# Attention plus MLP block on one core: a tenth of the exps on VectorE, one GELU per chunk, Q projections moved, denser fillers

## The chip, the cores and the metric

The kernel runs on 1 core of a Trainium2 chip. The time is device microseconds of that core. Executions of the kernel before span 0.4% in the main comparison (1060.83 to 1064.96 us) and 1.1% in the widest batch (1062.11 to 1073.93 us). The profiler names the engines PE (TensorE), DVE (VectorE), ACT (ScalarE), POOL (GpSimd) and SP (SyncE); PEld is TensorE's weight load.

## The reference

One transformer block on 2048 tokens of width 640, with modulation rows computed from a vector `c`. In what follows, a score product is a part of q k^T, an exp is the exponential of the softmax on such scores, and P.V is the product of the exps with v.

```python
qkv = (x @ wqkv).reshape(B, S, 3, H, Dh)          # H = 32 heads, Dh = 20
scores = einsum('bhqd,bhkd->bhqk', q, k) * Dh ** -0.5
o = einsum('bhqk,bhkd->bhqd', softmax(scores), v); attn = o.reshape(B, S, D) @ wo
...
x = x + ga * attn(layernorm(x) * (1 + ca) + sa)
h = gelu(y @ w1 + b1)                              # tanh form, F = 1536; y = layernorm(...)
x = x + gb * (h @ w2 + b2)
```

## The kernel before

The kernel builds a list of operations with their dependences. A list scheduler at build time puts them into a fixed order for each engine, and the order is then emitted with semaphores. Queries go in four chunks of 512. A chunk has 8 groups of 4 heads and 16 key tiles, which makes 2048 score tiles of 128x512 in all. While chunk i is in attention, TensorE also does projections (chunk 0) or the output product and the MLP of chunk i-1.

Score products of three tiles fill three PSUM banks (0 to 2, then 3 to 5), and one exp of 1536 columns empties them into a ring in SBUF (slots that are used again once P.V has read them). P.V accumulates in bank 6. Every other product ("auxiliary") goes through bank 7.

```python
def score_unit(ts, b0, prio=1):
    ...                                            # K = 32 products, one per tile, into banks b0..b0+2
    acts.append(P.op("act", lambda e: e.activation(dst, src, ACTF.Exp, scale=SCALE),
                     R=[pb], W=[dst], dur=d, lat=d + 0.24, prio=4, name="exp"))
```

A filler is a product with zero weights that adds nothing. It is there to keep TensorE's clock up, and the scheduler puts one in when TensorE would wait and too few columns were streamed lately:

```python
if be == "pe" and self.filler is not None and gate and bt > free["pe"] + 0.06:
    ...
    if sum(x[1] for x in fl) < self.fill_min:      # 3500 columns in the last 3.413 us
        o = self.op("pe", self.filler[0], ...)     # 512 columns into bank 6
```

`gate` is true only between the first and the last P.V row of a group. GELU is done piecewise: VectorE forms the argument for 1024 columns, ScalarE does a Tanh, VectorE the product; six times in each of chunks 0 to 2. All Q projections are done in chunk 0:

```python
late = [J_proj(g, 0, t) for t in (1, 2, 3) for g in range(NG)]   # 24 jobs of 5 products
```

The softmax here doesn't subtract the row's maximum and nothing guards it: scores larger than these inputs give would overflow.

Of the kernel before, what the change touches and what calls it, by code (L numbers as in the profile page):

```python
# [10 lines left out]
ESZ = {BF16: 2, F32: 4}  # L11


class Op:
    __slots__ = ("eng", "emit", "strong", "weak", "dur", "lat", "prio", "rel", "idx",
                 "users", "dma", "nbytes", "name", "npred", "ready", "t0", "t1",
                 "inc", "cnt", "sem", "startusers", "mode", "order", "wc", "gate")


class Sched:  # L20
# [10 lines left out]
    def __init__(self, nc, es):  # L31
        self.nc = nc
        self.ops = []
        self.marks = []
        self.filler = None
        self.fill_min = 3500
        self.lw = {}
        self.rd = {}
        self.fp = {}
        self.sem = {e: es.enter_context(nc.semaphore("s_" + e))  # L40
                    for e in ("pe", "act", "dve", "pool")}
        self.dsem = [es.enter_context(nc.semaphore(f"dm{i}")) for i in range(self.NDSEM)]
        self.ndma = 0
        self.dlast = [None] * self.NDSEM
# [35 lines left out]
    def op(self, eng, emit, R=(), W=(), dur=0.1, lat=None, prio=5, rel=None, name="",  # L80
           dma=False, nbytes=0, mode=0, after=(), wc=0.0, gate=None):
# [4 lines left out]
        o.wc, o.gate = wc, gate  # L86
# [33 lines left out]
        o.strong, o.weak = strong, weak - strong  # L120
        self.ops.append(o)
# [3 lines left out]
    def schedule(self):  # L125
# [17 lines left out]
        lastmode = {e: None for e in engs}  # L143
        bw = 0.0
        ham = {}
        fl = []
        gate = False
# [6 lines left out]
        while left:  # L154
# [7 lines left out]
            if be == "pe" and self.filler is not None and gate and bt > free["pe"] + 0.06:  # L162

                f0 = free["pe"]
                while fl and fl[0][0] < f0 - self.TICK:
                    fl.pop(0)
                if sum(x[1] for x in fl) < self.fill_min:
                    o = self.op("pe", self.filler[0], dur=self.filler[1] / 2400.0, mode="f", name="fill",
                                wc=float(self.filler[1]))
                    o.npred = 0  # L170
                    o.ready = 0.0
                    left += 1
                    avail["pe"].append(o)
                    bt = f0
# [5 lines left out]
            if be == "pe":  # L180
# [5 lines left out]
                if o.gate is not None:  # L186
                    gate = o.gate
                d *= slow
                if lastmode[be] != o.mode:
# [108 lines left out]
def bass_adaLN_cond__mha_block__mixer_channel_mlp__prompt_kernel(  # L298
# [8 lines left out]
    GELU_C = math.sqrt(2.0 / math.pi)  # L307
    X2, OUT2 = A_x[0], out[0]
    VW, RING = 24, 15
    QS = [(0, 512), (512, 512), (1024, 512), (1536, 512)]  # L310
    FILL = 760

    es = ExitStack()
    with es:
        P = Sched(nc, es)
        arena = es.enter_context(nc.sbuf_tensor("arena", [128, 98304], BF16))
# [3 lines left out]
        def V(off, shape, dtype=BF16):  # L320
# [4 lines left out]
            assert off % 64 == 0 and off + nb <= 196608, (off, nb)  # L325
# [9 lines left out]
        def alloc(nbytes):  # L335
            o = top[0]
            top[0] += (nbytes + 63) // 64 * 64
            assert top[0] <= 196608, top[0]
# [9 lines left out]
        o_ring = alloc(RING * 512 * 2)  # L348
        o_ot = alloc(2 * NG * 512 * 2)
        o_wo = alloc(NG * D * 2)  # L350
        o_mlp = alloc(8192)
# [7 lines left out]
        ring = V(o_ring, [RING * 512])  # L359
# [7 lines left out]
        x1b = V(o_mlp, [2, 1024])  # L367
        gsq = V(o_mlp + 4096, [1024])
        gth = V(o_mlp + 6144, [1024])
# [7 lines left out]
        b2b = V(o_ot + 13312, [D])  # L377
# [3 lines left out]
        gbh = V(o_mlp + 5120, [D])  # L381
        gab = V(o_mlp + 6400, [D])
# [4 lines left out]
        arena_t_f32 = rinv.tensor  # L387
        sumt = V(alloc(64), [16])
        rsm = V(alloc(64), [16], F32)
        zero = V(alloc(256), [128])  # L390
        gbb2 = V(alloc(1280), [D])
        sbr = V(alloc(1280), [D])
# [10 lines left out]
        b1col = V(alloc(64), [KF], F32)  # L403

# [23 lines left out]
        def mm(outp, lhsT, rhs, start, stop, prio, n, rel=None, name="", cyc=None):  # L428
# [3 lines left out]
                        name=name, wc=n)  # L432
# [29 lines left out]
        def mmjob(outp, pairs, n, prio, pace, name):  # L462
            rels = pace.rels(len(pairs))
            for i, (l, r) in enumerate(pairs):
                mm(outp, l, r, i == 0, i == len(pairs) - 1, prio, n, rel=rels[i], name=name)
# [11 lines left out]
        for w in (1, 0):  # L477
# [28 lines left out]
             dur=0.22, lat=0.4, prio=0, mode="f", name="warm", wc=512, gate=True)  # L506
        P.filler = (lambda e: e.matmul(bank(6), zero, idr, start=False, stop=False, skip_group_check=True), 512)  # L507
# [85 lines left out]

        def proj_job(g, which, tc, prio, pace=NOPACE, eng="dve"):
            bb = bank(aux_bank())
            mmjob(bb, [(wqk[:, kt, which, g * 128:(g + 1) * 128], hT[:, kt, tc * 512:(tc + 1) * 512])
                       for kt in range(KD)], 512, prio, pace, "proj")
            d = kT[:, g, tc * 512:(tc + 1) * 512] if which == 1 else qT[:, tc, g, :]
            if eng == "act":
                act(d, bb, ACTF.Copy, prio=1)  # L600
            else:
                dve(lambda e: e.tensor_copy(d, bb), [bb], [d], 512, prio=2)  # L602
# [18 lines left out]
        acts = P.marks  # L621
# [8 lines left out]
        def score_unit(ts, b0, prio=1):  # L630
# [19 lines left out]
            def em(e):  # L650
                r = None
                for (o_, lh, rh, hl) in lst:
# [6 lines left out]
                 wc=0.25 * n * len(ts))  # L659
# [3 lines left out]
            acts.append(P.op("act", lambda e: e.activation(dst, src, ACTF.Exp, scale=SCALE),  # L663
                             R=[pb], W=[dst], dur=d, lat=d + 0.24, prio=4, name="exp"))

        def pv_row(ci, g, kt, split=False):
# [10 lines left out]
            def em(e):  # L677
                r = None
                for (o_, lh, rh, hl) in lst:
# [5 lines left out]
                 gate=True if kt == 0 else False if kt == TT - 1 else None)  # L685
# [22 lines left out]
        def sum_job(ci, g):  # L708
# [15 lines left out]
            dve(lambda e: e.tensor_tensor(d, d, rb, op=ALU.mult), [d, rb], [d], n, prio=3, name="div")  # L724

        def attention(ci, g, kts, pend, two=False):
            n = QS[ci][1]
            for kt in kts:
                for hl in range(4):
                    if pend and pend[0][0] != ci and QS[pend[0][0]][1] != n:  # L730
                        score_unit(list(pend), 3 * (flat[0] % 2))
                        flat[0] += 1
                        pend.clear()
                    pend.append((ci, g, kt, hl))
                    k = 2 if two else 3 * (512 // n)
                    if len(pend) == k:
                        score_unit(list(pend), (2 if two else 3) * (flat[0] % 2))
                        flat[0] += 1
                        pend.clear()
# [29 lines left out]
        def run_chunk(ci, groups, aux):  # L769
# [3 lines left out]
            u0 = len(acts)  # L773
# [7 lines left out]
            for g in groups:  # L781
                for kt in range(TT):
                    attention(ci, g, [kt], pend)
                    todo.append((ci, g, kt))
                    while todo and (todo[0] + (3,)) in slot_of:
                        pv_row(*todo.pop(0))
                    flush(len(acts) - u0 - 1)
# [3 lines left out]
        aux = []  # L791

# [3 lines left out]
        def row_mod(dst, wm, c0, pace, scale=1.0, plus=0.0):  # L796

            for (n0, nw) in ((0, 512), (512, 128)):
# [6 lines left out]

        pool(lambda e: e.memset(selz, 0.0), [selz], prio=7)
        sz = selz.rearrange("p (a b) -> p a b", b=32)
        pool(lambda e: e.affine_select(out=sz, in_=sz, compare_op=ALU.not_equal, fill=1.0, base=-DH,
                                       pattern=[[-32, 4], [0, 32]], channel_multiplier=1),
             [selz], [selz], dur=0.3, prio=7)  # L810
# [6 lines left out]
        flat[0] = 0  # L817
        UG = 64 / 3.0
# [34 lines left out]
        def J_group(g):  # L853
            return [J_proj(g, 1, 0), J_proj(g, 0, 0), J_proj(g, 1, 1), J_proj(g, 1, 2), J_proj(g, 1, 3)]

        late = [J_proj(g, 0, t) for t in (1, 2, 3) for g in range(NG)]
        spread(0.5, UG - 1, mix(J_group(2), J_v(160) + [J_row(gab, wm1, 0)]))
        spread(UG, 2 * UG - 1, mix(J_group(3), J_v(320) + [
            J_row(sbr, wm1, D), J_row(cb1, wm2, 0, plus=1.0), J_row(gbh, wm2, D, scale=0.5), J_b1()]))
        spread(2 * UG, 3 * UG - 1, mix(J_group(4), J_v(480)))  # L860
        for i in range(3):
            spread((3 + i) * UG, (4 + i) * UG - 1, mix(J_group(5 + i), late[6 * i:6 * i + 6]))
        spread(6 * UG, 7 * UG - 3, late[18:])
# [8 lines left out]
        run_chunk(0, range(1, NG), aux)  # L872
        for g in range(NG):
            pool(lambda e, g=g: e.tensor_tensor(wo_pad[:, g, :], wo_pad[:, g, :], gab, op=ALU.mult),
                 [wo_pad[:, g, :]], [wo_pad[:, g, :], gab], dur=1.4, prio=7)
        pool(lambda e: e.tensor_tensor(gbb2, gbh, b2b, op=ALU.mult), [gbb2], [gbh, b2b], dur=1.4, prio=7)
        pool(lambda e: e.tensor_scalar_mul(gbb2, gbb2, 2.0), [gbb2], [gbb2], dur=1.8, prio=7)
# [24 lines left out]
        def ln2(ci, tl, tail=False):  # L902
# [16 lines left out]
            pool(lambda e: e.tensor_tensor(xt, xt, gbb2, op=ALU.add), [xt], [xt, gbb2], dur=1.4, prio=7)  # L919
# [10 lines left out]
        def m1_job(ci, ft, pace):  # L930
# [3 lines left out]
            ch = ft // 2  # L934
            d = x1b[:, ch % 2, (ft % 2) * n:(ft % 2 + 1) * n]
# [3 lines left out]
            if ft % 2 == 0:  # L939
                return  # L940
            w = 2 * n
            xv, q, t = x1b[:, ch % 2, 0:w], gsq[:, 0:w], gth[:, 0:w]
            dve(lambda e: e.tensor_tensor(q, xv, xv, op=ALU.mult), [xv], [q], w, mode=1.8, name="g1")
            dve(lambda e: e.tensor_scalar(q, q, 0.044715, 1.0, op0=ALU.mult, op1=ALU.add), [q], [q], w,
                mode=3.2, name="g2")
            dve(lambda e: e.tensor_tensor(q, q, xv, op=ALU.mult), [q, xv], [q], w, mode=1.8, name="g3")
            act(t, q, ACTF.Tanh, n=w, scale=GELU_C, prio=3, name="tanh")
            gv = g1T[:, 2 * ch:2 * ch + 2, 0:n]
            t3 = t.rearrange("p (f q) -> p f q", q=n)
            x3 = xv.rearrange("p (f q) -> p f q", q=n)  # L950
            dve(lambda e: e.scalar_tensor_tensor(out=gv, in0=t3, scalar=1.0, in1=x3, op0=ALU.add, op1=ALU.mult),  # L951
                [t3, x3], [gv], w, name="g4")
# [6 lines left out]
        def finish_y(ci, tl, half, bb, sc):  # L959
# [136 lines left out]
```

## Time and profile before

| what | value |
|---|---|
| time, median of 3 | 1064.37 us |
| span of the profiled run | 1059.2 us |
| ACT busy | 970.2 us (92%) |
| PE busy | 870.6 us (82%) |
| DVE busy | 316.7 us (30%) |
| mean granted clock of TensorE | 0.905 |

The page of the kernel before. Its first part is busy time (share of the span) and instructions, the second is busy tenths in 40 slices, the fourth is the chain of work that ended last.

```profile
PE 870.6 (82%) x6139; PEld 275.8 (26%) x6139; DVE 316.7 (30%) x595; ACT 970.2 (92%) x752; POOL 135.6 (13%) x173
...
DVE  6722232333124333211023243210034243210261
ACT  3799999999989999999999999999999999999632
...
PEclk9899999999968989988889999788899899897769
...
ACT 62%; PE 24%; DMA 7%; DVE 5%; POOL 1%; issue 1%; SPq 0%; POOLq 0%
```

ScalarE is at nine tenths or more from the 3rd to the 37th slice, but for one eight in the 12th, and 62% of the chain that ended last is ScalarE. This is the attention stage, from about 62 to 998 us. VectorE has room.

The timeline of ACT in the kernel before, at two places: start, duration, engine, source line, operation, number of instructions.

```profile
28.48 1.44 ACT L414 ACTIVATE arena<-psum,arena 128x512 bf16<-128x512 bf16 x2
...
597.65 13.63 ACT L663 ACTIVATE arena<-psum 128x1536 bf16<-128x1536 f32 x10
```

Start times in the trace's records make this exact. From the start of one 1536-column exp to that of the next (the cadence) the median is 1.330 us: 1280 ns of streaming and 50 ns more. (One column per cycle at 1.2 GHz, the Trainium skill says in "ScalarE: Activation LUTs", "What ACT_TABLE_LOAD costs", and the trace agrees: 1.330 us for 1536 columns and about 0.905 us for 1024 differ by 0.83 ns a column.) The ten exps above are nine such steps and the last one's own duration. The other line is two activations whose scale and bias are [128,1] operands in SBUF. Their starts lie 662 ns apart, 427 + 235. So two such operands cost 185 ns over an exp, which has neither.

From the first 1536-column exp to the end of the last exp the records give 930.9 us. At its medians ScalarE would need 661 x 1.330 = 879.1 us for the exps and 17.0 us for 18 Tanh. The other 34 us are lost between instructions. By the clock records 24 of them fall on exps that run at half clock.

The stretches view of the kernel before: busy time and instructions of each engine, then the granted clock, the DMA share and GB/s.

```profile
300.00:310.00 10.00, 10.00 (x54) 2.17 (x53) 2.33 (x5) 10.00 (x8) 8.29 (x9) 0.50 0.01 2
...
725.00:730.00 5.00, 5.00 (x26) 1.39 (x23) 0.00 (x0) 4.78 (x4) 0.00 (x0) 0.50 0.00 0
```

In the clock records the clock is 1.00 or 0.50, nothing between. It is 0.50 for 204 us in all (some 2 us of the record lie past the end of the span).

### The profile page before, as it was taken

What the parts mean: (1) busy time and instruction counts of PE and PEld (TensorE: products, weight loads), DVE (VectorE), ACT (ScalarE), POOL (GpSimd) and SP (SyncE); (2) the same over time, 40 slices, a digit from 0 to 9 for tenths busy, and PEclk for the clock granted to TensorE, in tenths of its full rate; (3) what the DMA queues carried; (4) which work ended last, traced back from release to release, by engine and by line L of the source; (5) the groups of instructions that cost most, each with busy time, mean ns of one, the idle gap of its engine ahead of it and who ended that gap; (6) DMA issues with size and microseconds to landing.
All of it is one profiled execution on the core that took longest, in us unless ns stands there. A gap on an engine that the chain in (4) does not pass through costs nothing.

```text
span 1059.2 us, 14000 instructions
## 1 busy us (share of the span) xinstructions
PE 870.6 (82%) x6139; PEld 275.8 (26%) x6139; DVE 316.7 (30%) x595; ACT 970.2 (92%) x752; POOL 135.6 (13%) x173
## 2 busy tenths in 40 slices
PE   6889888989888887788787887888887878788938
PEld 3433333222222222222222221222222222222315
DVE  6722232333124333211023243210034243210261
ACT  3799999999989999999999999999999999999632
POOL 4302110000086000000024100000024100000050
PEclk9899999999968989988889999788899899897769
DMA  9300000100400000100000000100000000000000
GB/s 322 102 12 7 5 11 12 36 11 12 150 18 8 6 11 12 36 17 23 17 2 11 11 11 11 60 17 20 12 11 11 11 12 11 11 17 17 13 1 25
DMA packets 28223, 29.77 MB, mean 28 GB/s; under 512 B 10626, under 2 KB 22274, under 8 KB 28162
## 3 DMA queue, kind: packets, MB, share of 16 engines
q1 hardware_dynamic: 26850, 28.67, 8.4%
q8 instruction: 48, 0.79, 0.3%
q10 hardware_dynamic: 1312, 0.20, 0.1%
q14 instruction: 13, 0.11, 0.0%
HBM read 25.87 MB, written 2.88 MB: 27 GB/s over the span
## 4 chain that ended last, share of the span: by engine, by line
ACT 62%; PE 24%; DMA 7%; DVE 5%; POOL 1%; issue 1%; SPq 0%; POOLq 0%
ACT arena L663 61%; PE psum L430 11%; PE psum L653 6%; PE psum L680 4%; DMA arena<-scr 3%; PE psum L507 2%; DMA scr<-arena 2%; ACT arena L414 1%; DMA arena<-arena 1%; DMA arena<-in_A_x_dram 1%; DVE arena L544 1%; DVE arena L562 1%; DVE arena L602 1%; DVE arena L618 1%; DVE arena L724 1%
## 5 line engine op out<-in xcount | busy, mean ns | idle before, releaser
L663 ACT ACTIVATE arena<-psum 128x1536 bf16<-128x1536 f32 (+2 forms) x694 | 931.2, 1569 | 22.1 <-PE psum L653 20.7
L653 PE MATMUL psum<-arena 32*128 32x512 bf16 x2048 | 292.3, 417 | 128.8 <-ACT arena L663 123.8
L430 PE MATMUL psum<-arena 128*128 128x512 bf16 (+3 forms) x1611 | 354.1, 329 | 32.6 <-DMA arena<-in_w_mod_dram 6.2
L680 PE MATMUL psum<-arena 128*32 128x512 bf16 (+1 forms) x2048 | 220.4, 422 | 0.4
L430 PEld LDWEIGHTS psum<-arena 128*128 128x128 bf16 x1611 | 125.9, 100 | 209.1 <-issue 104.2
L653 PEld LDWEIGHTS psum<-arena 32*128 32x128 bf16 x2048 | 67.8, 92 | 365.1 <-ACT arena L663 311.5
L507 PE MATMUL psum<-arena 128*128 128x512 bf16 x269 | 97.4, 444 | 0.0
L551 POOL TENSOR_SCALAR arena<-arena 128x1 f32<-128x1 f32 (+1 forms) x40 | 9.4, 236 | 641.1 <-DVE arena L546 640.7
L680 PEld LDWEIGHTS psum<-arena 128*32 128x32 bf16 (+1 forms) x2048 | 51.5, 93 | 133.3 <-issue 127.9
L602 DVE CAST arena<-psum 128x512 bf16<-128x512 f32 x63 | 43.5, 691 | 101.0 <-PE psum L430 101.0
L963 DVE SCALAR_TENSOR_TENSOR arena<-psum,arena 128x320 bf16<-128x320 f32 x32 | 15.7, 492 | 174.1 <-PE psum L430 174.1
L414 ACT ACTIVATE arena<-arena 128x1024 bf16<-128x1024 bf16 (+2 forms) x28 | 31.8, 1138 | 29.6 <-POOL arena L558 21.8
L724 DVE TENSOR_TENSOR arena<-arena 128x512 bf16<-128x512 bf16 x31 | 23.8, 767 | 108.6 <-DMA arena<-scr 108.6
L937 DVE TENSOR_SCALAR arena<-psum,arena 128x512 bf16<-128x512 f32 x36 | 26.9, 747 | 84.1 <-PE psum L430 84.1
L544 DVE BATCH_NORM_STATS2 arena<-arena 128x6 f32<-128x320 bf16 x96 | 44.0, 479 | 16.6 <-POOL arena L915 12.6
L982 POOL TENSOR_TENSOR arena<-arena 128x640 bf16<-128x640 bf16 x12 | 16.8, 1432 | 148.3 <-DMA arena<-in_B_w_dram 148.3
L436 PE MATMUL psum<-arena 128*128 128x128 bf16 (+2 forms) x162 | 17.4, 254 | 22.3 <-ACT arena L414 17.2
L688 DVE CAST arena<-psum 128x512 bf16<-128x512 f32 x32 | 22.1, 692 | 44.1 <-PE psum L680 43.8
L915 POOL TENSOR_TENSOR arena<-arena 128x640 bf16<-128x640 bf16 x24 | 33.4, 1393 | 7.4 <-DVE arena L562 7.4
L507 PEld LDWEIGHTS psum<-arena 128*128 128x128 bf16 x269 | 22.2, 104 | 41.2 <-issue 34.9
L895 DVE TENSOR_TENSOR arena<-psum,arena 128x320 bf16<-128x320 f32 x32 | 15.2, 484 | 57.1 <-PE psum L430 57.0
L951 DVE SCALAR_TENSOR_TENSOR arena<-arena 128x1024 bf16<-128x1024 bf16 x18 | 22.0, 1224 | 32.0 <-ACT arena L414 32.0
(49 smaller groups left out, 226.7 us busy)
## 6 DMA issues: line engine op xcount, KB each, us to landing
arena<-scr SPq DMA_DIRECT2D x31, 256.0 KB
arena<-in_A_x_dram SPq DMA_DIRECT2D x7, 640.0 KB, 11.2
arena<-in_B_w_dram SPq DMA_DIRECT2D x2, 1920.0 KB
arena<-in_w_mod_dram SPq DMA_DIRECT2D x2, 1600.0 KB
out_dram<-arena SPq DMA_DIRECT2D x16, 160.0 KB, 1.8
arena<-in_A_wqkv_dram SPq DMA_DIRECT2D x3, 800.0 KB
arena<-in_w_mod_dram SPq DMA_DIRECT2D x2, 800.0 KB
arena<-in_A_wo_dram SPq DMA_DIRECT2D x4, 200.0 KB
```

The costliest lines, as they stand in the source:

```text
L414: return P.op("act", lambda e: e.activation(outp, inp, func, **kw), R=[inp] + list(R), W=[outp], dur=d, lat=d + 0.2, prio=prio, name=name)
L430: return P.op("pe", lambda e: e.matmul(outp, lhsT, rhs, start=start, stop=stop), R=[lhsT, rhs], W=[outp], dur=d, lat=d + 0.17, prio=prio, ...
L507: P.filler = (lambda e: e.matmul(bank(6), zero, idr, start=False, stop=False, skip_group_check=True), 512)
L544: dve(lambda e, hf=hf, xi=xi: e.bn_stats(s6[:, hf, :], xi), [xi], [s6[:, hf, :]], 320, prio=prio, dur=0.39)
L602: dve(lambda e: e.tensor_copy(d, bb), [bb], [d], 512, prio=2)
L653: r = e.matmul(o_, lh, rh, start=True, stop=True, tile_position=(32 * hl, 0))
L663: acts.append(P.op("act", lambda e: e.activation(dst, src, ACTF.Exp, scale=SCALE), R=[pb], W=[dst], dur=d, lat=d + 0.24, prio=4, name="exp"))
L680: r = e.matmul(o_, lh, rh, start=(kt == 0), stop=(kt == TT - 1), tile_position=(0, 32 * hl))
L688: dve(lambda e: e.tensor_copy(d_, acc), [acc], [d_], n, prio=0, name="pvcopy")
L724: dve(lambda e: e.tensor_tensor(d, d, rb, op=ALU.mult), [d, rb], [d], n, prio=3, name="div")
L915: pool(lambda e, op=op, row=row: e.tensor_tensor(hd, hd, row, op=op), [hd], [hd, row], dur=1.4)
L937: dve(lambda e: e.tensor_scalar(d, bb, b_, None, op0=ALU.add), [bb, b_], [d], n, dur=0.1 + n / 900., prio=2, name="m1ev")
```

## The change

The intent is to take a tenth of the exps off ScalarE and give TensorE the means to keep up. Five parts, each cut to its core:

```diff
 # 1. the scores carry a shift of 22528, so that their fp32 bits hold the fraction of log2
+    QSC, QOF = SCALE * math.log2(math.e) * 128.0, 22528.0
+    # K row 20 of each head gets 1, Q row 20 gets 22528 (added when K and Q leave PSUM)
 # 2. the exps: 3 banks, then 2 banks; bank 5 is for tiles of VectorE; the shift is undone by a bias
-  e.activation(dst, src, ACTF.Exp, scale=SCALE)
+  e.activation(dst, src, ACTF.Exp, scale=ESC, bias=ebias)        # ebias: [128,1] column in SBUF
+  k = 2 if two or flat[0] % 2 else 3
 # 3. a tile on VectorE (188 of them: 0.31 per row of four tiles in chunk 0, 0.4 after)
+  dve(tensor_scalar_add(w_, m_, -65536.0))                       # m_: low 16 bits of the PSUM word
+  dve(tensor_tensor(w_, m_, w_, op=ALU.mult))
+  dve(scalar_tensor_tensor(out=w_, in0=m_, scalar=c2, in1=w_, op0=ALU.add, op1=ALU.mult))
+  dve(scalar_tensor_tensor(out=o_, in0=w_, scalar=al, in1=pb, op0=ALU.mult, op1=ALU.add))  # uint16 = bf16 bits
 # 4. GELU once per chunk, Q of chunks 2 and 3 in chunk 1
-  act(t, q, ACTF.Tanh, n=1024, ...)            # six times per chunk, with four VectorE products
+  e.activation(d, d, ACTF.Gelu_apprx_tanh)     # d: 12 x 512 columns
-  late = [J_proj(g, 0, t) for t in (1, 2, 3) for g in range(NG)]
+  q1 = [J_proj(g, 0, 1) for g in range(NG)]    # the other 16 jobs: slots 0.5 to 42 of chunk 1
 # 5. fillers: also inside five-product jobs and in the idle bank 7; a higher limit
-        self.fill_min = 3500
+        self.fill_min = 4500
-  ... and gate and bt > free["pe"] + 0.06:
-      if sum(x[1] for x in fl) < self.fill_min:
+  ... and (gates or idle) and bt > free["pe"] + 0.06:
+      if bt > f0 + 1.5 and f0 > 30.0 or sum(x[1] for x in fl) < self.fill_min:
```

Smaller parts: the row scaling after softmax goes from VectorE to GpSimd, and in the last chunk the addition of the bias row goes from GpSimd to VectorE, behind the transposes. The instruction order of both kernels shows what follows: exps go from 661 of 1536 columns and 32 of 1024 to 359 and 391, fillers from 269 to 701.

## The prediction

> **What bounds it now.** ScalarE. The page gives ACT 970 of 1059 us (92%), nine tenths or more through the attention stage (62 to 998 us); the chain of waits is 61% the exp line. The exps are 661 of 1536 columns, 32 of 1024 and one of 512. In the timeline nine exps take 12.1 us; start to start the median is 1.330 us for 1536 columns (50 ns over 1280 ns of streaming) and about 0.905 us for 1024. The floor of the stage is thus 662 x 1.33 + 18 Tanh x 0.945 = 897 us, against 936 us spent: some 35 us are lost between exps, about 22 of them while TensorE has half clock. The granted clock is 0.50 in stretches such as 300 to 310 us; the mean of 0.905 means some 200 us at half speed. The Trainium skill, "TensorE: Matmul & The Clock Gate", Part 1, says that a PE with too little activity falls to half clock, and this trace has exactly two values.
>
> **What the change does.**
> - 188 of 1984 score tiles leave ScalarE. For them VectorE gets a PSUM bank, so exps alternate 3 and 2 banks: 359 of 1536, 391 of 1024. At today's cadence that is 359 x 1.33 + 359 x 0.905 = 802 us instead of 880: -78 us.
> - But each exp now carries its bias as a [128,1] operand from SBUF; before, it was an immediate 0. The Trainium skill, "ScalarE: Activation LUTs", "What ACT_TABLE_LOAD costs", puts about 93 ns on each such operand. The trace agrees: back-to-back 512-column activations with two such operands start 662 ns apart, 427 + 235, where an exp adds 50: 92 ns each, not overlapped. 718 x 92 ns = +66 us. I expect it to show in full: 1.42 and 1.00 us start to start.
> - GELU: 18 Tanh (17 us of ACT) become 3 activations of 6144 columns (5.17 us) with two table loads each (1.28 us in this trace): about 24 us, +7.
> - VectorE: four more 512-column operations for each of 188 tiles. PSUM operations of this size take 0.69 to 0.75 us here, so 2.8 us per tile, +525 us; the GELU products (54 us) and the row scaling (24 us, now on GpSimd) go. VectorE rises from 317 to about 760 us, some 75%: busy but not the bound.
> - TensorE: fillers go from 269 to 701, 16 Q projections move to chunk 1, K=32 products come in smaller sets. Denser fillers should remove most half-clock stretches, so the 35 us lost between exps should fall to 15 or 20.
> - Tail: a 1.4 us GpSimd addition leaves the chain, some fillers come in: -3 us.
>
> **Sum.** 1061 - 78 + 66 + 7 - 17 - 3 = 1036 us; with some luck from the warmer clock, 1028. Range 980 to 1050. Faster by over 2%: 0.75; within 2%: 0.22; slower: 0.03.
>
> **What would show it.** Right: exps start to start near 1.42 and 1.00 us; ACT still over 90% busy; clock over 0.95; VectorE near 70 to 75% and seldom waited for; Gelu stops of about 8 us, three times. Wrong: cadence still 1.33 and 0.91 (the bias read is hidden; the time would be about 965 us); or idle gaps of ACT behind PE waiting for VectorE.
>
> **What would make it wrong.** The operand's cost being hidden in long activations (my evidence is from 512 columns with two of them); VectorE backlog where layer-norm statistics meet the off-loaded tiles, holding up TensorE in its fixed order; shorter two-bank exps leaving TensorE less time to refill three banks; the clock not rising.

## The result, and the profile after

| | before | after |
|---|---|---|
| time, median of 4 | 1063.72 us | 1027.99 us |
| span of the profiled run | 1059.2 us | 1024.6 us |
| ACT, PE, DVE busy | 92%, 82%, 30% | 94%, 93%, 70% |
| mean granted clock | 0.905 | 0.988 |
| half clock, total | 204 us | 26 us |

The ratio is 0.9666, 95% interval 0.9642 to 0.969. A ratio is the mean time of one kernel's fast runs over that of the other's of the same rounds, so not quite the ratio of the medians.

The page after:

```profile
PE 948.9 (93%) x6511; PEld 319.8 (31%) x6571; DVE 722.2 (70%) x1250; ACT 964.0 (94%) x800; POOL 163.0 (16%) x200
...
DVE  6677557687888888777688777467678777556171
ACT  4999999999999999999999999999999999999842
...
PEclk9999999999999999999999999999999999989979
...
ACT 77%; PE 14%; DVE 4%; DMA 3%; POOL 1%; issue 1%; SPq 0%
```

A tenth of the tiles has left ScalarE, and its busy time fell by only 6 us. The chain is still ScalarE's, even more so (77%).

The timeline of ACT after, around the first GELU:

```profile
403.35 17.23 ACT L728 ACTIVATE arena<-psum,arena 128x1536 bf16<-128x1536 f32 x14
420.60 1.28 ACT L1078 ACT_TABLE_LOAD   x1
421.89 5.32 ACT L1078 ACTIVATE arena<-arena 128x6144 bf16<-128x6144 bf16 x1
427.22 1.28 ACT L728 ACT_TABLE_LOAD   x1
428.51 3.98 ACT L728 ACTIVATE arena<-psum,arena 128x1536 bf16<-128x1536 f32 x3
```

The exps now name `arena` among their sources: that is the bias column. In the records a 1536-column exp takes 1.423 us to the next start and a 1024-column exp 0.996 us (medians); the first line is seven of each. The GELU stop runs from 420.60 to 428.51, 7.9 us.

The profiled runs, split by the records:

| part | before | after | difference |
|---|---|---|---|
| front, up to the first exp of 1536 columns | 67.5 | 61.5 | -6.0 |
| exps at their median cadence | 879.1 | 868.4 | -10.7 |
| GELU on ScalarE (Tanh, or function and loads) | 17.0 | 23.8 | +6.8 |
| lost between instructions of the stage | 34.1 | 15.3 | -18.8 |
| end, after the last exp | 60.9 | 54.8 | -6.1 |

One last exp of 512 columns, under 1 us in both, is left out. Of the gain of 34.6 us, moving exps gave 10.7, and GELU took most of that back. More than half is fewer gaps.

### The profile page after: what moved, and what is told of

It reads as the page before. It is cut to its first block, busy times and chain, and to the rows that moved or that the text cites. A ratio compares the mean times of both kernels' runs of the same rounds, so it can differ in the third digit from the quotient of the medians.

```text
span 1024.6 us, 15651 instructions
## 1 busy us (share of the span) xinstructions
PE 948.9 (93%) x6511; PEld 319.8 (31%) x6571; DVE 722.2 (70%) x1250; ACT 964.0 (94%) x800; POOL 163.0 (16%) x200
## 4 chain that ended last, share of the span: by engine, by line
ACT 77%; PE 14%; DVE 4%; DMA 3%; POOL 1%; issue 1%; SPq 0%
ACT arena L728 74%; PE psum L464 6%; PE psum L718 3%; PE psum L789 2%; PE psum L547 2%; ACT arena L1078 2%; DMA arena<-scr 1%; DMA arena<-in_A_x_dram 1%; DVE arena L600 1%; PE psum L745 1%; PE psum L470 1%; ACT arena L448 0%; DMA scr<-arena 0%; DVE arena L1029 0%; ACT L728 0%
## 5 line engine op out<-in xcount | busy, mean ns | idle before, releaser
L728 ACT ACTIVATE arena<-psum,arena 128x1536 bf16<-128x1536 f32 (+1 forms) x751 | 912.7, 1357 | 8.7 <-PE psum L718 5.6
L718 PE MATMUL psum<-arena 32*128 32x512 bf16 x1860 | 294.5, 385 | 42.3 <-ACT arena L728 32.6
L464 PE MATMUL psum<-arena 128*128 128x320 bf16 (+3 forms) x1551 | 318.8, 310 | 11.6 <-issue 2.9
L547 PE MATMUL psum<-arena 128*128 128x512 bf16 (+1 forms) x701 | 219.5, 393 | 0.2 <-issue 0.2
L789 PE MATMUL psum<-arena 128*32 128x512 bf16 (+1 forms) x2048 | 203.5, 390 | 0.8 <-ACT arena L728 0.6
L768 DVE TENSOR_SCALAR arena<-psum 128x512 f32<-128x512 uint16 x188 | 129.5, 689 | 99.7 <-PE psum L745 92.1
L464 PEld LDWEIGHTS psum<-arena 128*128 128x128 bf16 x1611 | 125.5, 97 | 161.1 <-issue 83.6
L772 DVE SCALAR_TENSOR_TENSOR arena<-arena,psum 128x512 uint16<-128x512 f32 x188 | 128.7, 685 | 65.7 <-PE psum L789 60.1
L718 PEld LDWEIGHTS psum<-arena 32*128 32x128 bf16 x1860 | 71.4, 91 | 263.8 <-ACT arena L728 237.5
L833 POOL TENSOR_TENSOR arena<-arena 128x512 bf16<-128x512 bf16 x31 | 36.0, 1162 | 670.8 <-DMA arena<-scr 670.8
L769 DVE TENSOR_TENSOR arena<-psum,arena 128x512 f32<-128x512 uint16 x188 | 129.2, 687 | 4.4
L770 DVE SCALAR_TENSOR_TENSOR arena<-psum,arena 128x512 f32<-128x512 uint16 x188 | 129.0, 686 | 4.1
L789 PEld LDWEIGHTS psum<-arena 128*32 128x32 bf16 (+1 forms) x2048 | 50.7, 91 | 124.4 <-issue 117.7
L547 PEld LDWEIGHTS psum<-arena 128*128 128x128 bf16 x701 | 58.0, 99 | 91.8 <-issue 70.0
L745 PE MATMUL psum<-arena 32*128 32x512 bf16 x188 | 71.9, 383 | 5.3 <-DVE arena L772 3.4
```

Of the source, the lines that this page charges most:

```text
L464: return P.op("pe", lambda e: e.matmul(outp, lhsT, rhs, start=start, stop=stop), R=[lhsT, rhs], W=[outp], dur=d, lat=d + 0.17, prio=prio, ...
L547: return lambda e: e.matmul(bank(b_)[:, 0:n_], zero, r_, start=new, stop=new, skip_group_check=True)
L718: r = e.matmul(o_, lh, rh, start=True, stop=True, tile_position=(32 * hl, 0))
L745: P.op("pe", lambda e: e.matmul(pb, lh, rh, start=True, stop=True, tile_position=(32 * hl, 0)), R=[lh, rh], W=[pb], dur=d, lat=d + 0.17, p ...
L768: dve(lambda e: e.tensor_scalar_add(w_, m_, -65536.0), [pb], [w_], n, prio=1, name="d1", dur=0.6)
L769: dve(lambda e: e.tensor_tensor(w_, m_, w_, op=ALU.mult), [pb, w_], [w_], n, prio=1, name="d2", dur=0.6)
```

## The experiments

Twelve kernels ran, each beside the kernel before on the same chip (experiments 5 to 8 on another chip than the other eight). The scheduler makes a new order in each build, so most edits also move fillers: there are 701 in the changed kernel, and 940 in experiment 4. "Lost" is always the excess over the median cadence in the attention stage of the profiled run.

### 1. The changed kernel with an immediate bias (e1_imm_bias)

```diff
+ # a second constant row: K row 21 = 1, Q row 21 = -16256, so ScalarE's scores hold 6272 and need no bias
- e.activation(dst, src, ACTF.Exp, scale=ESC, bias=ebias)
+ e.activation(dst, src, ACTF.Exp, scale=ESC)
- lh = kT[32 * hl:32 * hl + 32, ...]          # the tiles of VectorE
+ lh = kT[32 * hl:32 * hl + DH + 1, ...]      # leave row 21 out
```

> The changed kernel with one thing different: the bias of the exps is an immediate 0 again. The scores get their shift from a second constant row of the products (K row 1, Q row -16256), which the single VectorE tiles leave out, so the result should stay right and ScalarE's order is the same. Theory A (the [128,1] bias operand costs 92 ns of every exp, in full): exps 1.33 and 0.905 us start to start instead of 1.423 and 0.996, 750 x 92 ns = 69 us less ScalarE, and if ScalarE stays the bound 1028 - 69 = 959 us, say 955 to 975. Rival B (TensorE, now busy 93% of the span, or VectorE at 70% is as near to being the bound as ScalarE): the cadence floor falls but gaps open before the exps, and the time falls by less than half of that, to 995 us or more.

Result: correct, 998.75 us (ratio 0.9385 to before). The cadence fell to 1.347 and 0.908 us, near what theory A had: the floor, the time of all exps at their cadence, dropped by 59 us. (Experiment 7 has 1.330 and 0.904, so a part of 1.347 is waiting already; against those two the floor dropped by 66.) The time fell by only 29 us, which is rival B's side. The groups by form, of the changed kernel and then of this one:

```profile
L728 ACT ACTIVATE arena<-psum,arena 128x1536 bf16<-128x1536 f32 x359 | 566.8, 1579 | 6.1 <-PE psum L718 3.2 <-PE psum L789 1.8
L728 ACT ACTIVATE arena<-psum,arena 128x1024 bf16<-128x1024 f32 x391 | 449.0, 1154 | 2.7 <-PE psum L718 2.4
```

```profile
L739 ACT ACTIVATE arena<-psum 128x1536 bf16<-128x1536 f32 x359 | 525.1, 1463 | 24.9 <-PE psum L800 13.3 <-PE psum L729 8.3
L739 ACT ACTIVATE arena<-psum 128x1024 bf16<-128x1024 f32 x391 | 404.0, 1037 | 10.6 <-PE psum L729 10.2
```

The last columns are idle time of ScalarE just before these exps, and what ended it: the P.V products (L800, which free ring slots; L789 in the changed kernel) and the score products (L729; L718). More than half of the idle before the three-bank exps ends at a P.V product, so the refill of banks is not the only limit. By the records 43 us are lost after two-bank exps, against 14 in the changed kernel: while a two-bank exp runs, TensorE has 0.91 us to refill three banks. The operand's price is real, and it was paying for slack that TensorE needed.

### 2. The kernel before with a bias operand (e2_before_ptr)

```diff
- e.activation(dst, src, ACTF.Exp, scale=SCALE)
+ e.activation(dst, src, ACTF.Exp, scale=SCALE, bias=ebias)   # a zero column in SBUF
```

> The kernel before with one thing different: its exps take their bias (zero) from a [128,1] column in SBUF. Same order on all engines. Theory A: 1.422 us start to start instead of 1.330, so 694 x 92 ns = 64 us more ScalarE; part of the 34 us lost between exps is absorbed, since TensorE has more time per exp, so 1063 + 64 - 10 to 20 = 1107 to 1117 us. Rival (the longer cadence of the changed kernel comes from something else in it, for instance PSUM shared with VectorE): no change, 1063 us.

Result: correct, 1110.90 us (ratio 1.0437), as theory A said. Nothing else of the change is in this kernel, and the median cadence is 1.423 us. The floor rose by 61 us; the loss fell from 34 to 21 us at even less clock (258 us at half).

### 3. The changed kernel with the old fill rule (e3_old_fill)

```diff
-  self.fill_min = 4500
+  self.fill_min = 3500
-  while fl and fl[0][0] < min(bt, f0 + 1.0) - self.TICK:
+  while fl and fl[0][0] < f0 - self.TICK:
-  gate = (7, n if i == 0 else 0)         # fillers inside five-product jobs
+  gate = None
-  idle = bool(deps) and all(...)         # fillers in the free auxiliary bank
+  idle = False
-  if bt > f0 + 1.5 and f0 > 30.0 or sum(x[1] for x in fl) < self.fill_min:
+  if sum(x[1] for x in fl) < self.fill_min:
```

> The changed kernel with the fill rule of before (limit 3500 columns, filler only between the first and last P.V row of a group): 142 fillers instead of 701. Theory (the denser fillers keep TensorE at full clock, and that is what removed about 20 us of gaps between exps and the 6 us each before and after the stage): half-clock time rises from 26 us to over 150 us, gaps return, 1028 + 15 to 30 = 1043 to 1058 us. Rival (the gaps went because the longer exps with the operand leave TensorE more time, whatever its clock): half clock returns but the time changes by less than 5 us.

Result: correct, 1080.02 us (ratio 1.0159, 95% interval 1.0115 to 1.0203): slower than the kernel before, by less than 2%. That is 52 us over the changed kernel, where I expected 15 to 30. The stretches view of this kernel and, in the second fence, of the changed one:

```profile
640.00:680.00 40.00, 35.69 (x171) 7.17 (x174) 25.22 (x38) 33.38 (x27) 2.33 (x2) 0.62 0.14 42
680.00:730.00 50.00, 42.62 (x192) 9.02 (x192) 21.19 (x34) 41.38 (x31) 1.16 (x1) 0.52 0.04 13
```

```profile
640.00:680.00 40.00, 37.01 (x233) 12.03 (x233) 21.69 (x35) 39.80 (x30) 1.16 (x1) 1.00 0.12 39
680.00:730.00 50.00, 48.25 (x339) 15.68 (x338) 34.31 (x55) 49.95 (x43) 2.32 (x2) 1.00 0.07 22
```

The fourth busy figure is ACT. At clock 0.52 it did 31 activations in 50 us, at 1.00 it did 43. Half clock lasted 330 us in all, and 54 us were lost after two-bank exps: 46 of them after the 92 that ran at half clock, 8 after the 267 at full clock. The 87 three-bank exps at half clock lost 6 us.

### 4. The changed kernel with no tile on VectorE (e4_no_offload)

```diff
- run_chunk(0, range(1, NG), aux, lambda s: (0.31, 0.0))
+ run_chunk(0, range(1, NG), aux, lambda s: (0.0, 0.0))
- run_chunk(ci, range(NG), aux, lambda s: (0.4, 0.0))
+ run_chunk(ci, range(NG), aux, lambda s: (0.0, 0.0))
```

> The changed kernel with no tile moved to VectorE (share 0): all 1984 tiles go to ScalarE in sets of 3 and 2, bias operand as in the changed kernel. Theory (ScalarE is the bound, and a tile moved saves its ScalarE time of 2.419 us per 5 tiles = 484 ns and costs nothing elsewhere): 188 x 0.484 = 91 us more, about 1028 + 91 - 5 = 1110 to 1120 us. Rival (the off-loaded tiles cost waits that eat part of the gain: the 14 us lost after two-bank exps): 1028 + 91 - 15 or lower, 1085 to 1105 us.

Result: correct, 1118.30 us (ratio 1.0507), 90 us over the changed kernel. This is the theory's 91: a moved tile is worth its full ScalarE time, and the loss after two-bank exps is about the same without it (15 us).

### 5. The kernel before with the new fill rule (e5_before_newfill)

The edit is part 5 of the change, put into the kernel before: 979 fillers instead of 269.

> The kernel before with only the new fill rule (limit 4500 columns, filler also inside the five-product jobs and in the free auxiliary bank): 979 fillers instead of 269. Theory (the denser fillers are nearly the whole gain; exps moved, bias operand and GELU cancel to about 5 us of ScalarE floor): half clock nearly gone, the 34 us lost between exps fall to about 10, the front loses 5 us: 1063 - 24 - 5 = about 1034 us, 1025 to 1045. Rival (the fillers help only together with the rest, since the old kernel's gaps are not from the clock, or 979 fillers stand in the way of score products): 1055 us or more.

Result: correct, 1048.12 us (ratio 0.9857, 95% interval 0.982 to 0.9893). It lies between theory and rival. Half clock went from 204 to 26 us, yet 21 us stayed lost. The first two stretches of the kernel before and then of this one:

```profile
62.00:300.00 238.00, 208.25 (x1593) 70.36 (x1591) 66.65 (x109) 230.80 (x172) 23.96 (x17) 0.98 0.09 29
300.00:530.00 230.00, 189.10 (x1287) 52.47 (x1286) 61.47 (x109) 224.13 (x168) 30.32 (x34) 0.88 0.05 16
```

```profile
62.00:300.00 238.00, 215.42 (x1638) 74.95 (x1662) 67.09 (x109) 230.37 (x170) 22.55 (x16) 1.00 0.09 30
300.00:530.00 230.00, 215.04 (x1518) 67.27 (x1524) 62.41 (x110) 228.65 (x173) 31.69 (x35) 1.00 0.05 16
```

The first stretch holds chunk 0, whose exps end at about 273 us, and the start of chunk 1. Its clock had been 0.98 already, and ACT is busy 230 of 238 us in both. In the stretches after it, gaps of more than 60 ns over the median summed to 22 us before and to 4 us here. So the clock cost gaps in chunks 1 to 3, and something else costs 11 to 15 us up to 300 us.

The traces show a part of that. At 294 us both kernels have their longest gap of this stretch (3.2 us before, 3.7 us here): TensorE stands 3.5 and 3.8 us at an output product that is next in its order, until VectorE has scaled the rows after softmax, for which VectorE waits for sums that go through DRAM. The chain that ended last in the kernel before goes through it (start, us, what):

```profile
276.41 7.48 DMA arena<-arena
284.19 6.48 DMA scr<-arena
290.69 4.76 DMA arena<-scr
295.47 1.12 DVE arena L724
```

The half clock from 294 to 315 us sets in during this stop, so it did not cause it. In the changed kernel, where GpSimd does that scaling and 16 Q projections come at this place, the stop is gone; which of the two removed it was not tested.

### 6. Tanh in the place of the GELU function (e6_gelu_as_tanh)

```diff
- e.activation(d, d, ACTF.Gelu_apprx_tanh)
+ e.activation(d, d, ACTF.Tanh)              # wrong on purpose; no table loads
```

> The changed kernel with Tanh in the place of the tanh-GELU function in the three activations of 6144 columns: wrong result on purpose, same sizes and order, but no table loads around them. Theory (ScalarE is the bound, so six loads of 1.295 us are paid in full): 1028 - 7.8 = 1020 us. Rival (TensorE and VectorE use these stops to catch up, so that part of the 7.8 us comes back as fewer gaps): 1024 us or more.

Result: 1027.56 us (ratio 0.9671), so no visible gain in the time. (The comparison passed it as correct, presumably because the MLP branch is small in this output.) In the profiled run the stage is 4.5 us shorter than in the changed kernel, with 4 us more lost, as the rival had it. The front, however, was 67.8 us instead of 61.5 with the same program, so the total can't settle it. Inconclusive in the time; what the trace shows is that the loads are taken in full on ScalarE and about half comes back.

### 7. Immediate bias, fill limit 3500 (e7_imm_fill3500)

```diff
-  self.fill_min = 4500
+  self.fill_min = 3500                     # on top of experiment 1
```

> The immediate-bias kernel with the fill limit at 3500 columns instead of 4500, the places of fillers as in the changed kernel: 361 fillers instead of 701. Theory C (with short exps TensorE's fixed order is crowded, and fillers in it are what delays the score products after two-bank exps): the 43 us lost there fall to under 30, 998 - 15 = about 983 us. Rival D (the delay comes from the useful products, and fillers only keep the clock): half clock comes back and the time rises, to 1005 us or more.

Result: correct, median 1003.78 us, but the four runs spread from 989.65 to 1008.10 us. Two of them are called slow, as over 1.5% above the fastest; the ratio of the other two is 0.9365 (95% interval 0.9288 to 0.9442). The time goes roughly with the mean clock: 0.983 for 989.65, 0.971 for 1000.65, 0.961 for the profiled 1006.90, 0.964 for 1008.10. In the profiled run half clock lasted 80 us, and 59 us were lost, against 42 in experiment 1: with fewer fillers the gaps did not shrink, as theory C would have it, but the clock fell too. It doesn't decide between C and D.

### 8. Immediate bias, fillers cut to the gap (e8_imm_fitfill)

```diff
+  gn = min(gn, max(192, int((bt - f0) * 2400.0) // 32 * 32))   # and none for gaps under 80 ns
```

> The immediate-bias kernel with each filler cut to the gap that the scheduler sees (192 to 512 columns, none for gaps under 80 ns), limit 4500 as before. Theory C (a 512-column filler put into a shorter gap delays the next score product by up to 0.15 us): gaps fall by about 10 us at unchanged clock, 985 to 992 us. Rival D: within 3 us of 998.

Result: correct, 990.10 us (ratio 0.9316), the time that theory C gave. The clock stayed (0.99). But the loss in the stage fell only from 42 to 37 us, half of theory C's 10; the other 7 us between the two profiled runs are the front (66.8 and 59.6 us), which theory C doesn't speak of and which differed by as much between two kernels with the same front program (61.5 and 67.8 us, the changed kernel and experiment 6). So the fitted fillers are worth some 5 us as far as the traces show. This is the best version: 7% under the kernel before and 4% under the changed one.

### 9. More tiles on VectorE (e9_imm_fit_more)

```diff
- (0.31, 0.0)   (0.4, 0.0)                  # tiles per row: chunk 0, later chunks
+ (0.38, 0.0)   (0.49, 0.0)                 # on top of experiment 8: 230 tiles instead of 188
```

> The immediate-bias kernel with fitted fillers and more tiles moved: 230 instead of 188 (733 exps instead of 750). VectorE then rises from about 73% to 86% of the span. Theory (ScalarE's exps still bound it): 42 tiles x 0.449 us = 19 us less, 990 - 19 = 971 us, at least 12 us of it. Rival (the gaps before the exps, from TensorE's crowded order and its waits for VectorE, have become the bound): 985 us or more.

Result: correct, 1034.83 us (ratio 0.9711): 45 us slower than with 188 tiles, far beyond the rival. The waits view of experiment 8 and, in the second fence, of this one: who waited for whom, us in total, times, longest.

```profile
PEld psum L757 <- DVE arena L784: 28.6, 81, 1.4
...
ACT arena L740 <- PE psum L801: 10.5, 34, 1.0
```

```profile
ACT arena L740 <- PE psum L801: 63.8, 76, 2.8
...
PEld psum L757 <- DVE arena L784: 49.1, 108, 1.4
```

TensorE now stands 49 us before off-loaded score products (L757) until VectorE's last step (L784) frees bank 5, and ScalarE stands 64 us for P.V (L801) to free ring slots. VectorE is busy 81% on average, and most of the loss is at 300 to 400, 500 to 650 and 750 to 900 us, where layer norm and the MLP's evictions run on it too. That VectorE's backlog causes the whole 45 us is argued, not shown: the wait for it grew by 21 us, and the scheduler also placed other fillers.

### 10. The addition back on GpSimd at the end (e10_tail_pool_add)

```diff
-            if not tail:
-                pool(... tensor_tensor(xt, xt, gbb2, op=ALU.add) ...)
+            pool(... tensor_tensor(xt, xt, gbb2, op=ALU.add) ...)
-        # four VectorE additions after the transposes
```

> The changed kernel with the four additions of the bias row in the last chunk put back on GpSimd, inside the layer-norm chain, as in the kernel before. Theory (these additions, 1.4 to 1.7 us each in front of the next small GpSimd steps, are what shortened the end of the kernel by 6 us): the time from the last exp to the end goes from 54.7 back to 59 or 60 us, 1028 + 4 to 5 = 1032 to 1033 us. Rival (the end is shorter because of the fillers' clock): under 1.5 us.

Result: correct, 1031.74 us (ratio 0.9684). The time from the last exp to the end went from 54.8 to 59.7 us. The timeline of GpSimd in this kernel shows the four additions among the small layer-norm steps:

```profile
982.83 1.65 POOL L1053 TENSOR_TENSOR arena<-arena 128x640 bf16<-128x640 bf16 x1
...
984.92 1.39 POOL L1053 TENSOR_TENSOR arena<-arena 128x640 bf16<-128x640 bf16 x1
...
986.70 1.68 POOL L1053 TENSOR_TENSOR arena<-arena 128x640 bf16<-128x640 bf16 x1
...
992.58 1.39 POOL L1053 TENSOR_TENSOR arena<-arena 128x640 bf16<-128x640 bf16 x1
```

### 11. No tile on VectorE and the old fill rule (e11_no_offload_old_fill)

The edit is that of experiments 3 and 4 together.

> The changed kernel with no tile on VectorE and with the fill rule of before: sets of 3 and 2 banks, 235 fillers. It asks why the old fill rule costs 52 us in the changed kernel when new fillers gain only 15 us in the old one. Theory S (it is the two-bank exps: at half clock TensorE cannot refill three banks within one of them): like the changed kernel with the old rule, 40 us or more are lost after two-bank exps, 1118 + 35 = 1150 us or more. Rival V (it is the off-loaded tiles: their single products and the waits for VectorE stand in TensorE's fixed order): the loss stays near 20 to 25 us, 1118 + 5 to 15 = 1123 to 1133 us.

Result: correct, 1192.71 us (ratio 1.1197). Without any off-loaded tile the old rule costs 74 us, with them 52, so the tiles are not why. Half clock lasts 505 us, and 72 us are lost after two-bank exps, against 15 in experiment 4. Of the 72 us, 67 fall on 164 two-bank exps at half clock; 163 three-bank exps at half clock lost 6. The kernel before with long exps of three banks (experiment 2) lost 21 us with 258 us of half clock. So it is the short turn of the 3-and-2 split that needs the full clock.

### 12. All Q projections in chunk 0 (e12_q_in_chunk0)

```diff
+  q1 += [J_proj(g, 0, t) for t in (2, 3) for g in range(NG)]   # spread over the last four groups of chunk 0
-  for i in range(16):
-      add_k(0.5 + 2.6 * i, 2.6, ...)                           # chunk 1
```

> The changed kernel with all Q projections in chunk 0 again (16 jobs of five products moved back out of chunk 1). Theory (at full clock TensorE has room for them in either place): within 3 us of 1028. Rival (chunk 0 has no room; moving them out was worth about what the half-clock stretch at 294 to 315 us cost before): 1033 us or more.

Result: correct, 1040.74 us (ratio 0.9772), 13 us over the changed kernel, as the rival had it. The stretches view of (roughly) chunk 0 here and, in the second fence, in the changed kernel:

```profile
62.00:270.00 208.00, 188.54 (x1374) 66.21 (x1395) 135.14 (x213) 192.26 (x158) 20.37 (x16) 1.00 0.05 13
```

```profile
62.00:260.00 198.00, 184.28 (x1362) 64.18 (x1386) 139.12 (x219) 196.41 (x161) 20.35 (x16) 1.00 0.05 14
```

The clock is 1.00 in both. ScalarE idles 16 us of chunk 0 with the Q products there, under 2 us without. The waits of ScalarE for score products, here and in the changed kernel:

```profile
ACT arena L728 <- PE psum L718: 18.7, 13, 6.8
```

```profile
ACT arena L728 <- PE psum L718: 5.6, 8, 1.2
```

Two stops of 6.9 and 4.8 us, at 242 and 207 us, make most of it. In both TensorE runs projections one after the other, and before each waits for VectorE to empty the one auxiliary bank; the next score products stand behind them in its order. So it isn't the sum of the products that doesn't fit, but a row of them that comes due at once, at full clock too. Whether the 24 late Q projections do the same in the kernel before was not tested: its chunk 0 lost 7 us (10 with the new fill rule), without such a stop, and under the longer exps of experiment 2 only 2, with all Q projections in it.

## Why the prediction was right or wrong

The time, 1027.99 us, is the one forecast, but partly by luck: the sum of my terms was 1036, and 8 us were a hedge "with some luck". What filled it in the profiled run is 6 us of front, for which I had no term, and 3 us more of the end than I had.

- **The bias operand: right, and shown.** I said 1.42 and 1.00 us start to start; the trace has 1.423 and 0.996. Experiment 2 puts the operand alone into the kernel before and gets 1.423 from 1.330; experiment 1 takes it out of the changed kernel. What I did not see is that it also bought slack: taking it out saves 59 us of exps and 29 us of time, since the loss rises from 15 to 42 us.
- **Exps moved: right.** Forecast -78 + 66 = -12, measured -10.7 at the cadences. Experiment 4 gives 90 us for the 188 tiles.
- **GELU: right in size on ScalarE** (+7 forecast, +6.8 measured). Experiment 6 did not find it in the total time.
- **VectorE: right.** Forecast 760 us and some 75%, measured 722 us and 70%. At this share it isn't the bound; experiment 9 shows that there is little room above it.
- **Lost time: right in size, the cause right only in part.** I wrote that "denser fillers should remove most half-clock stretches, so the 35 us lost between exps should fall to 15 or 20". It fell from 34 to 15. For the 24 us at half clock the mechanism held: with the fillers alone (experiment 5) under 2 us of loss fall on half clock. But 19 us are lost there at full clock. Of these 15 lie before 300 us, where the changed kernel loses under 5. Three things that I had not priced can account for that: longer exps (experiment 2: the operand alone takes the loss from 34 to 21 us), the place of 16 Q projections (experiment 12: 13 us), and the wait for the row scaling at 294 us. My own example of slow TensorE, 300 to 310 us, comes right after that stop. How the gain splits among the three is not shown.
- **The weight of the fillers: underrated.** "Some 17 us" was their share in my sum. In the changed kernel they are worth 52 us (experiment 3): without them the change would be a loss of 1.6%. Sets of two banks leave TensorE about 1 us to refill three, and at half clock that fails (experiments 3 and 11).
- **The end: under half.** I said -3 us, with one addition leaving the chain. It is four additions; the end shrank by 6.1 us, and experiment 10 gives 4.9 of them back.
- **The front: not foreseen, and not shown to be the change's.** It was 6 us shorter in the profiled run. Over all profiled runs of kernels with the new fill rule the front took 59.6 to 62.5 us in those whose clock was full from 25 to 41 us, and 64.6 to 67.8 in those with a half-clock window there, whatever else was changed (the same front program gave 61.5 and 67.8). All four profiled runs with the old rule had such a window (65.8 to 67.5 us), and four of the ten with the new rule. Whether the change makes it rarer stays open.

## What to carry to other kernels

When work leaves the bounding engine, price what the remaining instructions of that engine take on: here 92 ns per exp for one operand ate some 66 of 78 us; a constant row in a product that runs anyway did the same work, and 29 us came back. An engine in fixed order needs slack against the shortest interval it must serve, not against the average; shorter intervals make the kernel depend on things (the clock, a crowded chunk) that longer ones hid. Before crediting a gap to the clock, look whether the gaps lie where the clock was low, and which came first.

## What the Trainium skill lacked or had wrong

- "ScalarE: Activation LUTs", "What ACT_TABLE_LOAD costs": the figure of about 93 ns for a [128,1] operand agrees. The page gives it for the length of one activation and doesn't say whether it stays in a back-to-back stream of long ones. It does: 1.423 us against 1.330 for 1536 columns from PSUM, back to back. The stated overlap of 93 ns between activations is too small for immediates: 186 ns of fixed cost shrink to 50 ns here, an overlap of 136.
- The same section gives about 2.66 us for a switch of table sets. Here a load takes 1.295 us to the next start, and both switches around a GELU together cost 2.9 us (0.14 to 0.24 + 1.295 before it, 0.115 + 1.295 after it), about 1.45 us each.
- "TensorE: Matmul & The Clock Gate", Part 1: the advice with a figure is about idle gaps of over 3.4 us; shorter idling is mentioned without one. In the kernel before the clock fell 23 times in the attention stage, and in the 3.4 us before each fall the longest stretch without a product in flight was 0.4 to 1.5 us. What separated the windows best is how much was streamed. I counted columns (a quarter for products on 32 rows or 32 columns) over the 8192 cycles that the page's 2.4 GHz and 3413 ns make of a window: 0.22 to 0.39 before a fall, 0.34 to 0.77 with nine tenths above 0.41 where the clock stayed full. The page has no such figure. The changed kernel's median is 0.58.
- No page says how short the interval between evictions may be before a TensorE in fixed order falls behind; in this kernel, with 0.91 us to refill three banks, 43 us were lost in 359 turns, and with 0.996 us 14 (experiment 1 and the changed kernel).
